# First row tiles by two PSUM tiles, early weights in four large pieces, and smaller moves in a fused attention and gated feed-forward kernel

## Chip, core, metric

One core of one Trainium2 chip. The metric is device time in microseconds (us) of one execution; every kernel was compared with the reference in each run and was correct. All executions used are with a granted TensorE clock of 0.998 to 1.0. PE is TensorE, DVE is VectorE, ACT is ScalarE and SP is SyncE; PSUM is where the kernel puts the results of its matmuls.

## The reference, cut to what matters

```python
xn = _layernorm(x)                      # x: 2048 x 640
s  = attention(xn @ wq, k, v) @ wo      # 32 heads of 192, last 512 keys
g  = silu((silu(xn @ w_gate) * (xn @ w_up)) @ w_down)     # F = 1536
return x + s * g
```

## The kernel before: the parts concerned

Rows are worked in 4 blocks of 4 tiles of 128. For block 0 the kernel normalizes each tile, transposes it by TensorE into PSUM, copies it to `xnT`, and starts the gate and up products (steps f = 0 to 2) tile by tile while weights still arrive. The rest of block 0 (f = 3 to 11) takes 512 columns at a time. Then come blocks 1 to 3, whose rows are transposed by DMA, and the 16 head pairs of the attention. A context is one head pair with one block of 512 rows; its matmuls are mostly row-tiled, that is, they come in pairs of 64 rows each.

```python
load_x(0)                  # in two halves, on SP's and ACT's queue
load_x(1, nc.scalar)
for cs in (slice(0, 1), slice(1, 3), slice(3, NC)):       # first quarter of w_gate, w_up
    if cs.stop == NC: load_x(2)
    for eng, w_sb, w in ((nc.sync, wg_sb, B_w_gate), (nc.scalar, wu_sb, B_w_up)): ...
load_x(3); load_gu(1)
for t in range(4, 8): load_x(t)
load_gu(2); load_gu(3); ...
# [cut]
def ready(t):
    ln_transpose(t)                                       # 5 chunks into one PSUM tile
    n = NC if t else 2
    nc.scalar.copy(xnT[:, 0:n, rows], tps[t][:, 0:n, :])
    if n < NC: nc.vector.tensor_copy(out=xnT[:, n:NC, rows], in_=tps[t][:, n:NC, :])
# [cut] in the loop over blocks b and steps f, for the next block's rows
if nx and 1 <= f < 5: ln_stats(4 * b + 3 + f) ...
if nx and 5 <= f < 9:
    ln_apply(4 * b + f - 1)
    ln_transpose_dma(4 * b + f - 1)
# [cut] attention: query projection of the next context; drop() does the last half
# of an output tile that was held back from the context before
for c in range(NC):
    if c == NC - 1 and between: between()
# [cut] division of a context: first query tile on DVE, second on ACT, if i < 2
```

The softmax here doesn't subtract the row's maximum and nothing guards it: scores larger than these inputs give would overflow.

Of the kernel before, what the change touches and what calls it, by code (L numbers as in the profile page):

```python
# [15 lines left out]
def kernel(  # L16
# [13 lines left out]
    nc = tc.nc  # L30
# [35 lines left out]
    wpool = ctx.enter_context(tc.tile_pool(name="att_w", bufs=2))  # L66
    kpool = ctx.enter_context(tc.tile_pool(name="att_k", bufs=1))
    qpool = ctx.enter_context(tc.tile_pool(name="att_q", bufs=2))
    psum = ctx.enter_context(tc.tile_pool(name="psum", bufs=2, space=bass.MemoryType.PSUM))

    def sc_tile():
        return psum.tile([P, 2, 512], f32, name="sc", tag="sc")

    def mm_tile():
        return psum.tile([P, 2, 512], f32, name="mm", tag="mm")


    ctx.enter_context(tc.manual_schedule())
# [86 lines left out]
    with ExitStack() as fctx:  # L165
# [13 lines left out]

        def load_x(t, eng=nc.sync):  # L180
            x_t[t] = lnx.tile([P, D], bf, name="x_t")
            if t == 0:
                for r, eng in ((lo, nc.sync), (hi, nc.scalar)):
                    eng.dma_start(out=x_t[t][r, :], in_=x2[t * P + r.start : t * P + r.stop, :])
            else:
                eng.dma_start(out=x_t[t][:], in_=x2[t * P : (t + 1) * P, :])

        def load_gu(q):
            cols = slice(q * FQ, (q + 1) * FQ)
# [4 lines left out]
                out=wu_sb[:, :, cols], in_=B_w_up[:, cols].rearrange("(c p) f -> p c f", p=P)  # L194
            )

        load_x(0)
        load_x(1, nc.scalar)
        for cs in (slice(0, 1), slice(1, 3), slice(3, NC)):
            if cs.stop == NC:  # L200
                load_x(2)
            for eng, w_sb, w in ((nc.sync, wg_sb, B_w_gate), (nc.scalar, wu_sb, B_w_up)):
                src = w[cs.start * P : cs.stop * P, 0:FQ].rearrange("(c p) f -> p c f", p=P)
                eng.dma_start(out=w_sb[:, cs, 0:FQ], in_=src)
        load_x(3)
        load_gu(1)
        for t in range(4, 8):
            load_x(t)
        load_gu(2)
        load_gu(3)  # L210
        nc.sync.dma_start(out=wd_sb[:], in_=B_w_down.rearrange("(f p) d -> p f d", p=P))


        nc.scalar.activation(act_t[:], one_t[:], ACT.Sqrt)
        warm = sc_tile()

        def keep_warm(n):
            for _ in range(n):
                nc.tensor.matmul(warm[:, 0, :], zero_t[:, 0:P], zero_t[:], start=True, stop=True)

        keep_warm(11)

        def ln_stats(t, between=None):
            b, ti = divmod(t, 4)
# [30 lines left out]
                    op0=ALU.subtract, op1=ALU.mult,  # L255
                )

        tps = {}

        def ln_transpose(t):  # L260
            xn = xns.pop(t)
            tps[t] = tp[:, t % 2, 0 : NC * P].rearrange("p (c k) -> p c k", c=NC)
            for c in range(NC):
                nc.tensor.transpose(tps[t][:, c, :], xn[:, c * P : (c + 1) * P], ident[:])

        def ln_transpose_dma(t):
            nc.sync.dma_start_transpose(
                out=xnT[:, 0:NC, t * P : (t + 1) * P], in_=xns.pop(t)[:]
            )
# [13 lines left out]
            nc.scalar.activation(sg[:], g, ACT.Silu)  # L283
            nc.vector.tensor_tensor(hTs[b][:, f, :], u, sg[:], ALU.mult)  # L284

        def ffn_hidden(b, f):
            gu = mm_tile() if (b, f) == (0, 3) else sc_tile()
            for s in range(2):
                hidden_mm(gu[:, s, :], s, f, slice(b * 512, (b + 1) * 512))
            hidden_gate(b, f, gu[:, 0, :], gu[:, 1, :])  # L290

        def ffn_down(b, u):
            ti, n = divmod(u, 2)
# [23 lines left out]
        hTs[0] = ffh.tile([P, NF, 512], bf, name="hT")  # L317


        first = {f: [sc[:, s, :] for s in range(2)] for f, sc in ((0, sc_tile()), (1, sc_tile()))}  # L320
        tp = psum.tile([P, 2, 1024], bf, name="tp", tag="mm")
        first[2] = [mm[:, s, :] for mm in (mm_tile(),) for s in range(2)]
        def ready(t):
            ln_transpose(t)
            rows = slice(t * P, (t + 1) * P)
            n = NC if t else 2
            nc.scalar.copy(xnT[:, 0:n, rows], tps[t][:, 0:n, :])
            if n < NC:
                nc.vector.tensor_copy(out=xnT[:, n:NC, rows], in_=tps[t][:, n:NC, :])

        ln_stats(0)
        ln_sqrt(0)
        ln_stats(1, lambda: ln_apply(0, (slice(0, 2 * P), slice(2 * P, D))))
        ready(0)
        ln_sqrt(1)
        keep_warm(3)
        banks = [(f, s) for f in range(3) for s in range(2)]
        for t in range(4):
            rows = slice(t * P, (t + 1) * P)

            order = [(*fs, [c]) for c in range(NC) for fs in banks]
            if t:
                order = [(*fs, range(NC)) for fs in banks]
            for k, (f, s, cs) in enumerate(order):
                if k == len(order) * 3 // 5 and t < 3:
                    if t == 1:
                        ln_stats(3, lambda: ln_apply(2))
                    else:
                        ln_apply(t + 1)
                    ready(t + 1)  # L350
                    if t == 0:
                        ln_stats(2)
                    if t < 2:
                        ln_sqrt(t + 2)
                    else:
                        nc.scalar.activation(act_t[:], one_t[:], ACT.Silu)
                hidden_mm(first[f][s][:, rows], s, f, rows, cs)
                if t == 3 and s == 1:
                    hidden_gate(0, f, *first[f])
        nc.gpsimd.memset(V_p[:, :, :, Dh : Dh + 2], 1.0)  # L360

        for b in range(NB):
            if b:
                hTs[b] = ffh.tile([P, NF, 512], bf, name="hT")
            nx = b + 1 < NB
            u = 0
            for f in range(NF):
                if nx and b and f == 0:
                    for t in range(4 * b + 4, 4 * b + 8):
                        load_x(t)  # L370
                if b or f >= 3:
                    ffn_hidden(b, f)
                if nx and 1 <= f < 5:
                    ln_stats(4 * b + 3 + f)
                    if f == 4:
                        ln_rstd(b + 1, 0, 4)
                if nx and 5 <= f < 9:
                    ln_apply(4 * b + f - 1)
                    ln_transpose_dma(4 * b + f - 1)

                if b >= 1 and f % 3:
                    ffn_down(b - 1, u)
                    u += 1
                if b == 2:
                    if f == 0:
                        load_k(0)
                    elif 2 <= f < 6:
                        transpose_k(0, f - 2)
                    elif f == 6:
                        load_wq(0)  # L390
                    elif 7 <= f < 10:
                        sum_k(0, f - 7)
                elif b == 3:
                    if f < 5:
                        centre_k(0, f)
                    elif f < 8:
                        (load_k, load_wq, load_wo)[f - 5]((1, 1, 0)[f - 5])
# [23 lines left out]
    def q_rows(i, j, between=None):  # L421
        pr, b = divmod(i, NB)
        if i not in qTs:
            qTs[i] = qpool.tile([P, 3, 512], bf, name="qT")
        q_ps = mm_tile()
        for c in range(NC):
            if c == NC - 1 and between:
                between()
            for h, r in enumerate((lo, hi)):
                nc.tensor.matmul(  # L430
                    q_ps[:, h, :], pairs[pr]["wq"][r, c, j * P : (j + 1) * P], xnT[r, c, b * 512 : (b + 1) * 512],
                    start=(c == 0), stop=(c == NC - 1),
                )
        with nc.allow_low_precision(reason="a sum of two, rounded once, like a copy out of PSUM"):
            nc.vector.reduce_sum(  # L435
                qTs[i][:, j, :], q_ps[:, :, :].rearrange("p h n -> p n h"), axis=AX.X
            )
# [13 lines left out]
    def pv(i, q2):  # L451
# [4 lines left out]
        def part(p):  # L456
            if p == 0:
                if q2 == 0:
                    Obs[i] = opool.tile([P, 4, 2, Dh], bf, name="O_b")
                    tag = "OT_l" if late(i) and pr < last else "OT_b"  # L460
                    OTs[i] = otpool.tile([P, 12, P], bf, name=tag, tag=tag, bufs=2 if tag == "OT_l" else 3)
                st["alone"] = i < 2 or (pr == last and 2 * b + q2 < 5)
                st["acc"] = sc_tile() if st["alone"] and q2 and b < 2 else mm_tile()
            acc = st["acc"]
            turn, h = divmod(p, 2)
            for kc in range(KC):
# [10 lines left out]
            if p == 1:  # L477
                turned(m, st)
            if p == 3:
                divide(i, q2, acc, st["alone"])  # L480

        return [lambda p=p: part(p) for p in range(4)]

    def divide(i, q2, acc, alone):
        pr, b = divmod(i, NB)
        O_b, OT_b = Obs[i], OTs[i]
        r = smpool.tile([P, 2, 2, 1], f32, name="r")
# [2 lines left out]
        for k in range(2):  # L490
            qt = 2 * q2 + k
            a_k = a_v[:, k, :, :]
            if k == 0 and alone:
                nc.vector.tensor_tensor(
                    O_b[:, qt, :, :], a_k[:, :, 0:Dh], r[:, k, :, :].to_broadcast([P, 2, Dh]),
                    ALU.mult,
                )
                continue
# [9 lines left out]
    def pv_full(i, q2):  # L508
# [4 lines left out]
            tag = "OT_l" if late(i) and pr < last else "OT_b"  # L513
            OTs[i] = otpool.tile([P, 12, P], bf, name=tag, tag=tag, bufs=2 if tag == "OT_l" else 3)
        O_b, OT_b = Obs[i], OTs[i]
        alone = i < 2 or (pr == last and 2 * b + q2 < 5)
        acc = sc_tile() if alone and b == 1 else mm_tile()
        for k in range(2):
            qt = 2 * q2 + k
            for h in range(2):  # L520
                for kc in range(KC):
# [2 lines left out]
                        Ps[i][kc][:, h, qt * P : (qt + 1) * P], V_p[:, kc, h, 0 : Dh + 1],  # L524
                        start=(kc == 0), stop=(kc == KC - 1),
                    )
        divide(i, q2, acc, alone)

    def load_xr(t):
        xrs[t] = finp.tile([P, D], bf, name="x_r", bufs=8)  # L530
# [243 lines left out]
```

## Time and profile before

| | before |
|---|---|
| median of 6 executions | 924.16 us (923.96 to 924.82) |
| the profiled one, its span | 924.28, 922.5 us |
| first matmul on real weights | 6.88 us |
| first 512-column matmul of block 0 | 15.69 us |
| PE busy from 203 to 915 us | 711.95 of 712.00 us |

A row of the order of time is start, duration (of a merged group: from its first start to its last end), engine, line, operation, tiles, count, and in brackets the idle time of the engine before it with what ended it. A row of the chain of waits is start, duration, and what the end of the program hung on just then. The records of matmuls overlap: 64-row ones of 512 columns are shown as 376 ns long, though pairs follow each other every 216 ns. Rows between those shown are left out of the fences.

### The profile page before, as it was taken

How to read it: one execution, taken by the hardware profiler on the slowest of the kernel's cores; microseconds unless marked ns; L12 is line 12 of the kernel's file. 1: busy time of each engine (PE TensorE's matmuls, PEld its weight loads, DVE VectorE, ACT ScalarE, POOL GpSimd, SP SyncE). 2: the span in 40 equal slices, each digit the busy share in tenths (PEclk: the TensorE clock that was granted, in tenths of full speed). 3: DMA queues.
4: the chain of work that ended last, by engine and by line, in shares of the span. 5: the costliest groups of instructions: out<-in, count | busy, mean ns of one | idle time of the engine just before them, and what ended most of it. 6: DMA issues, size and time to landing. Idle time of an engine off the chain costs nothing.

```text
span 922.5 us, 25778 instructions
## 1 busy us (share of the span) xinstructions
PE 915.9 (99%) x11085; PEld 624.4 (68%) x11101; DVE 575.7 (62%) x847; ACT 473.7 (51%) x847; POOL 101.6 (11%) x390
## 2 busy tenths in 40 slices
PE   9999999999999999999999999999999999999998
PEld 5455555575858586868686767676777777676666
DVE  6433331467676767676666667676767676767656
ACT  4222223556464656555556565655555555556561
POOL 0000000000000000000000000000000000002978
PEclk9999999999999999999999999999999999999999
DMA  9321510044544434444536262525271817163534
GB/s 293 78 53 35 114 35 1 1 74 93 88 78 83 83 79 88 72 93 65 102 57 109 55 112 53 113 45 121 41 125 36 131 37 123 32 124 92 120 71 141
DMA packets 243810, 77.18 MB, mean 84 GB/s; under 512 B 224624, under 2 KB 243696, under 8 KB 243696
## 3 DMA queue, kind: packets, MB, share of 16 engines
q1 hardware_dynamic: 242640, 74.73, 41.7%
q8 instruction: 87, 1.43, 0.7%
q10 hardware_dynamic: 1056, 0.80, 0.3%
q14 instruction: 27, 0.22, 0.1%
HBM read 39.45 MB, written 2.62 MB: 46 GB/s over the span
## 4 chain that ended last, share of the span: by engine, by line
PE 98%; DMA 1%; DVE 0%; ACTq 0%; issue 0%; POOLq 0%; POOL 0%; DVEq 0%
PE mm L430 22%; PE sc L567 19%; PE sc L444 18%; PE mm L470 16%; PE sc L276 11%; PE mm L298 6%; PE sc L539 3%; PE mm L522 2%; PE mm L539 1%; DMA wu_sb<-in_B_w_up_dram 1%; PE mm L276 0%; PE mm L311 0%; PE sc L470 0%; PE sc L522 0%; PE mm L444 0%
## 5 line engine op out<-in xcount | busy, mean ns | idle before, releaser
L448 ACT ACTIVATE p_t<-sc 128x1024 bf16<-128x1024 f32 x254 | 252.9, 1022 | 128.6 <-PE sc L444 128.6
L435 DVE TENSOR_REDUCE qT<-mm 128x512 bf16<-128x1024 f32 x189 | 231.0, 1223 | 92.5 <-PE mm L430 90.0
L500 ACT ACTIVATE O_b<-mm,r 128x192 bf16<-128x192 f32 x486 | 164.6, 421 | 183.4 <-issue 161.3
L430 PE MATMUL mm<-xnT,wq_p 64*128 64x512 bf16 x1890 | 240.1, 376 | 0.0
L592 DVE TENSOR_TENSOR sacc<-sacc,sc 128x640 f32<-128x640 f32 x200 | 164.3, 821 | 89.4 <-PE sc L567 89.4
L567 PE MATMUL sc<-wo_p,OT_b 64*128 64x320 bf16 x2592 | 217.2, 296 | 0.0
L444 PE MATMUL sc<-qT,khat 64*128 64x512 bf16 x1524 | 198.2, 376 | 0.1
L470 PE MATMUL mm<-V_p,p_t 64*128 64x193 bf16 x3520 | 186.3, 243 | 0.0
L470 PEld LDWEIGHTS <-p_t 64*128 64x128 bf16 x3584 | 162.6, 93 | 12.5 <-issue 0.4
L430 PEld LDWEIGHTS <-wq_p 64*128 64x128 bf16 x1890 | 105.2, 94 | 95.0 <-issue 0.5
L567 PEld LDWEIGHTS <-OT_b 64*128 64x128 bf16 x2592 | 140.1, 94 | 21.6
L444 PEld LDWEIGHTS <-khat 64*128 64x128 bf16 x1536 | 85.5, 94 | 79.4 <-issue 0.4
L555 POOL MEMSET turn_t<- 128x1 f32 x328 | 32.2, 98 | 696.4 <-PE mm L470 474.0
L284 DVE TENSOR_TENSOR hT<-sc,sg 128x512 bf16<-128x512 f32 x46 | 31.7, 690 | 85.2 <-ACT sg L283 85.1
L283 ACT ACTIVATE sg<-sc 128x512 bf16<-128x512 f32 x46 | 27.3, 596 | 72.4 <-PE sc L276 72.4
L276 PE MATMUL sc<-xnT,wu_sb 128*128 128x512 bf16 (+1 forms) x259 | 59.1, 355 | 0.3 <-DMA wu_sb<-in_B_w_up_dram 0.3
L276 PE MATMUL sc<-xnT,wg_sb 128*128 128x512 bf16 (+1 forms) x248 | 58.6, 354 | 0.6
L298 PE MATMUL mm<-wd_sb,hT 128*128 128x320 bf16 x384 | 56.6, 299 | 0.0
L489 DVE RECIPROCAL r<-mm 128x4 f32<-128x4 f32 x124 | 22.7, 183 | 47.4 <-PE mm L470 36.0
L298 PEld LDWEIGHTS <-hT 128*128 128x128 bf16 x384 | 37.5, 98 | 19.0
L276 PEld LDWEIGHTS <-wu_sb 128*128 128x128 bf16 x285 | 26.3, 98 | 27.2 <-DMA wu_sb<-in_B_w_up_dram 0.4
L276 PEld LDWEIGHTS <-wg_sb 128*128 128x128 bf16 x285 | 26.4, 98 | 23.2 <-DMA wg_sb<-in_B_w_gate_dram 0.2
(69 smaller groups left out, 373.8 us busy)
## 6 DMA issues: line engine op xcount, KB each, us to landing
wo_p<-in_A_wo_dram SPq DMA_DIRECT2D x16, 480.0 KB, 4.2
K_p<-in_A_k_cache_dram SPq DMA_DIRECT2D x32, 192.0 KB, 3.3
V_p<-in_A_v_cache_dram SPq DMA_DIRECT2D x32, 192.0 KB, 3.0
wq_p<-in_A_wq_dram SPq DMA_DIRECT2D x64, 80.0 KB, 3.1
wq_p<-in_A_wq_dram SPq DMA_DIRECT2D x16, 160.0 KB, 3.3
x_r<-in_A_x_dram SPq DMA_DIRECT2D x16, 160.0 KB, 4.1
x_t<-in_A_x_dram SPq DMA_DIRECT2D x14, 160.0 KB, 3.0
OT_b<-O_b SPq DMA_TRANSPOSE x124, 2.9
```

The costliest lines, as they stand in the source:

```text
L276: nc.tensor.matmul(out, w_sb[:, c, f * P : (f + 1) * P], xnT[:, c, qc], start=(c == 0), stop=(c == NC - 1),)
L298: nc.tensor.matmul(dn[:, 0:HD], hTs[b][:, f, ti * P : (ti + 1) * P], wd_sb[:, f, cols], start=(f == 0), stop=(f == NF - 1),)
L430: nc.tensor.matmul(q_ps[:, h, :], pairs[pr]["wq"][r, c, j * P : (j + 1) * P], xnT[r, c, b * 512 : (b + 1) * 512], start=(c == 0), stop=(c ...
L435: nc.vector.reduce_sum(qTs[i][:, j, :], q_ps[:, :, :].rearrange("p h n -> p n h"), axis=AX.X)
L444: nc.tensor.matmul(sc[:, h, :], khat[r, j, ks], qT[r, j, :], start=(j == 0), stop=(j == 2))
L448: nc.scalar.activation(p_t[:, :, :], sc[:, :, :], ACT.Exp, scale=scale)
L470: m = nc.tensor.matmul(acc[:, k, h * 256 : h * 256 + Dh + 1], Ps[i][kc][r, h, qt * P : (qt + 1) * P], V_p[r, kc, h, 0 : Dh + 1], start=(p ...
L500: nc.scalar.activation(O_b[:, qt, h, :], a_k[:, h, 0:Dh], ACT.Copy, scale=r[:, k, h, :])
L539: nc.tensor.matmul(ps, OTs[i][:, 3 * qt + j, :], pairs[i // NB]["wo"][:, j, cols], start=(first and j == 0), stop=(end and j == 2),)
L555: st["turn"] = nc.gpsimd.memset(turn_t[:], 0.0)
L567: m = nc.tensor.matmul(ps[:, n, 0:HD], OTs[i][r, 3 * qt + j, :], pairs[i // NB]["wo"][r, j, n * HD : (n + 1) * HD], start=(turn == 0 and j ...
L592: nc.vector.tensor_tensor(s_t, s_t, sc[:, :, 0:HD], ALU.add)
```

## The change

Its intent: let PE begin tile 0 after two of five transposes; fetch the early weights in fewer, larger transfers; put the weights of steps 6 to 8 ahead of rows not yet needed; and spare contexts 0 and 1 the hand-over from DVE to ACT within one division. With it come a new place for the transposes in a tile (four fifths), next block's layer norm one step later, and the held part one chunk earlier.

```diff
+        def load_first(cs):
+            for w_sb, w in ((wg_sb, B_w_gate), (wu_sb, B_w_up)):
+                nc.sync.dma_start(out=w_sb[:, cs, 0:FQ], in_=src)
-        load_x(0)
+        load_x(0, nc.scalar)
         load_x(1, nc.scalar)
-        for cs in (slice(0, 1), slice(1, 3), slice(3, NC)): ...
+        load_first(slice(0, 2))
+        load_first(slice(2, NC))
+        load_x(2)
         load_x(3)
         load_gu(1)
+        load_gu(2)
         for t in range(4, 8):
             load_x(t)
-        load_gu(2)
# [cut: pools; warming on zeros of 9 long and 6 short matmuls, none after the transposes]
+            for tp, cs in zip(tps, PARTS):        # chunks 0-1 and 2-4, a PSUM tile each
+                for k, c in enumerate(range(cs.start, cs.stop)):
+                    nc.tensor.transpose(tp[:, k, :], xn[:, c * P : (c + 1) * P], ident[:])
# [cut: copies by part on ACT; the last part of tile 3 on DVE]
-            if t:
+            if t == 3:
                 order = [(*fs, range(NC)) for fs in banks]
-                if k == len(order) * 3 // 5 and t < 3:
+                if k == len(order) * 4 // 5 and t < 3:
# [cut: step 3 ahead of the loop]
-                if nx and 1 <= f < 5:
-                    ln_stats(4 * b + 3 + f)
+                if nx and 2 <= f < 6:
+                    ln_stats(4 * b + 2 + f)
-                if nx and 5 <= f < 9:
+                if nx and 6 <= f < 10:
-            if c == NC - 1 and between:
+            if c == NC - 2 and between:
-                divide(i, q2, acc, st["alone"])
+                divide(i, q2, acc, (0, 1) if i < 2 and q2 == 0 else ())
```

More of the change, by code (lines that the diff above doesn't have):

```diff
@@ L68 @@
     qpool = ctx.enter_context(tc.tile_pool(name="att_q", bufs=2))
-    psum = ctx.enter_context(tc.tile_pool(name="psum", bufs=2, space=bass.MemoryType.PSUM))
+    sc_pool = ctx.enter_context(tc.tile_pool(name="psum_sc", bufs=2, space=bass.MemoryType.PSUM))
+    mm_pool = []
     def sc_tile():
-        return psum.tile([P, 2, 512], f32, name="sc", tag="sc")
+        return sc_pool.tile([P, 2, 512], f32, name="sc")
     def mm_tile():
-        return psum.tile([P, 2, 512], f32, name="mm", tag="mm")
+        return mm_pool[0].tile([P, 2, 512], f32, name="mm")
     ctx.enter_context(tc.manual_schedule())
@@ L181, in load_x @@
             x_t[t] = lnx.tile([P, D], bf, name="x_t")
-            if t == 0:
-                for r, eng in ((lo, nc.sync), (hi, nc.scalar)):
-                    eng.dma_start(out=x_t[t][r, :], in_=x2[t * P + r.start : t * P + r.stop, :])
-            else:
-                eng.dma_start(out=x_t[t][:], in_=x2[t * P : (t + 1) * P, :])
+            eng.dma_start(out=x_t[t][:], in_=x2[t * P : (t + 1) * P, :])
+        def load_first(cs):
+            for w_sb, w in ((wg_sb, B_w_gate), (wu_sb, B_w_up)):
+                src = w[cs.start * P : cs.stop * P, 0:FQ].rearrange("(c p) f -> p c f", p=P)
+                nc.sync.dma_start(out=w_sb[:, cs, 0:FQ], in_=src)
         def load_gu(q):
@@ L195, in load_gu, with keep_warm @@
             )
-        load_x(0)
+        load_x(0, nc.scalar)
         load_x(1, nc.scalar)
-        for cs in (slice(0, 1), slice(1, 3), slice(3, NC)):
-            if cs.stop == NC:
-                load_x(2)
-            for eng, w_sb, w in ((nc.sync, wg_sb, B_w_gate), (nc.scalar, wu_sb, B_w_up)):
-                src = w[cs.start * P : cs.stop * P, 0:FQ].rearrange("(c p) f -> p c f", p=P)
-                eng.dma_start(out=w_sb[:, cs, 0:FQ], in_=src)
+        load_first(slice(0, 2))
+        load_first(slice(2, NC))
+        nc.scalar.activation(act_t[:], one_t[:], ACT.Sqrt)
+        load_x(2)
         load_x(3)
         load_gu(1)
+        load_gu(2)
         for t in range(4, 8):
             load_x(t)
-        load_gu(2)
         load_gu(3)
         nc.sync.dma_start(out=wd_sb[:], in_=B_w_down.rearrange("(f p) d -> p f d", p=P))
-        nc.scalar.activation(act_t[:], one_t[:], ACT.Sqrt)
-        warm = sc_tile()
-        def keep_warm(n):
-            for _ in range(n):
-                nc.tensor.matmul(warm[:, 0, :], zero_t[:, 0:P], zero_t[:], start=True, stop=True)
-        keep_warm(11)
+        early = ExitStack()
+        psum1 = early.enter_context(tc.tile_pool(name="psum1", bufs=1, space=bass.MemoryType.PSUM))
+        PARTS = (slice(0, 2), slice(2, NC))
+        tps = [psum1.tile([P, 8, P], bf, name="tp", tag="tp%d" % n) for n in range(2)]
+        first = [
+            [gu[:, s, :] for s in range(2)]
+            for gu in (sc_tile(), sc_tile(), psum1.tile([P, 2, 512], f32, name="gu"))
+        ]
+        def keep_warm(n, cols=512):
+            for _ in range(n):
+                nc.tensor.matmul(
+                    first[2][1][:, 0:cols], zero_t[:, 0:P], zero_t[:, 0:cols], start=True, stop=True
+                )
+        keep_warm(9)
+        keep_warm(6, P)
         def ln_stats(t, between=None):
@@ L256, in ln_apply @@
                 )
-        tps = {}
-        def ln_transpose(t):
-            xn = xns.pop(t)
-            tps[t] = tp[:, t % 2, 0 : NC * P].rearrange("p (c k) -> p c k", c=NC)
-            for c in range(NC):
-                nc.tensor.transpose(tps[t][:, c, :], xn[:, c * P : (c + 1) * P], ident[:])
         def ln_transpose_dma(t):
@@ L284, in hidden_gate, with ffn_hidden @@
             nc.vector.tensor_tensor(hTs[b][:, f, :], u, sg[:], ALU.mult)
-        def ffn_hidden(b, f):
-            gu = mm_tile() if (b, f) == (0, 3) else sc_tile()
+        def ffn_hidden(b, f, gu=None):
+            gu = gu or [sc[:, s, :] for sc in (sc_tile(),) for s in range(2)]
             for s in range(2):
-                hidden_mm(gu[:, s, :], s, f, slice(b * 512, (b + 1) * 512))
-            hidden_gate(b, f, gu[:, 0, :], gu[:, 1, :])
+                hidden_mm(gu[s], s, f, slice(b * 512, (b + 1) * 512))
+            hidden_gate(b, f, *gu)
         def ffn_down(b, u):
@@ L317 @@
         hTs[0] = ffh.tile([P, NF, 512], bf, name="hT")
-        first = {f: [sc[:, s, :] for s in range(2)] for f, sc in ((0, sc_tile()), (1, sc_tile()))}
-        tp = psum.tile([P, 2, 1024], bf, name="tp", tag="mm")
-        first[2] = [mm[:, s, :] for mm in (mm_tile(),) for s in range(2)]
         def ready(t):
-            ln_transpose(t)
-            rows = slice(t * P, (t + 1) * P)
-            n = NC if t else 2
-            nc.scalar.copy(xnT[:, 0:n, rows], tps[t][:, 0:n, :])
-            if n < NC:
-                nc.vector.tensor_copy(out=xnT[:, n:NC, rows], in_=tps[t][:, n:NC, :])
+            xn, rows = xns.pop(t), slice(t * P, (t + 1) * P)
+            for tp, cs in zip(tps, PARTS):
+                for k, c in enumerate(range(cs.start, cs.stop)):
+                    nc.tensor.transpose(tp[:, k, :], xn[:, c * P : (c + 1) * P], ident[:])
+            for tp, cs in zip(tps, PARTS):
+                part = tp[:, 0 : cs.stop - cs.start, :]
+                if t == 3 and cs.stop == NC:
+                    nc.vector.tensor_copy(out=xnT[:, cs, rows], in_=part)
+                else:
+                    nc.scalar.copy(xnT[:, cs, rows], part)
         ln_stats(0)
@@ L335 @@
         ln_sqrt(1)
-        keep_warm(3)
         banks = [(f, s) for f in range(3) for s in range(2)]
@@ L359 @@
                     hidden_gate(0, f, *first[f])
+        ffn_hidden(0, 3, [psum1.tile([P, 512], f32, name="gu3", tag="tp%d" % n)[:, :] for n in range(2)])
+        early.close()
+        mm_pool.append(ctx.enter_context(tc.tile_pool(name="psum_mm", bufs=2, space=bass.MemoryType.PSUM)))
         nc.gpsimd.memset(V_p[:, :, :, Dh : Dh + 2], 1.0)
@@ L370 @@
                         load_x(t)
-                if b or f >= 3:
+                if b or f >= 4:
                     ffn_hidden(b, f)
-                if nx and 1 <= f < 5:
-                    ln_stats(4 * b + 3 + f)
-                    if f == 4:
+                if nx and 2 <= f < 6:
+                    ln_stats(4 * b + 2 + f)
+                    if f == 5:
                         ln_rstd(b + 1, 0, 4)
-                if nx and 5 <= f < 9:
-                    ln_apply(4 * b + f - 1)
-                    ln_transpose_dma(4 * b + f - 1)
+                if nx and 6 <= f < 10:
+                    ln_apply(4 * b + f - 2)
+                    ln_transpose_dma(4 * b + f - 2)
                 if b >= 1 and f % 3:
@@ L461, in part @@
                     OTs[i] = otpool.tile([P, 12, P], bf, name=tag, tag=tag, bufs=2 if tag == "OT_l" else 3)
-                st["alone"] = i < 2 or (pr == last and 2 * b + q2 < 5)
-                st["acc"] = sc_tile() if st["alone"] and q2 and b < 2 else mm_tile()
+                st["acc"] = sc_tile() if i < 2 and q2 else mm_tile()
             acc = st["acc"]
@@ L479, in part, with divide @@
             if p == 3:
-                divide(i, q2, acc, st["alone"])
+                divide(i, q2, acc, (0, 1) if i < 2 and q2 == 0 else ())
         return [lambda p=p: part(p) for p in range(4)]
-    def divide(i, q2, acc, alone):
+    def divide(i, q2, acc, by_dve):
         pr, b = divmod(i, NB)
@@ L492, in divide @@
             a_k = a_v[:, k, :, :]
-            if k == 0 and alone:
+            if by_dve and k in by_dve:
                 nc.vector.tensor_tensor(
@@ L515, in pv_full @@
         O_b, OT_b = Obs[i], OTs[i]
-        alone = i < 2 or (pr == last and 2 * b + q2 < 5)
+        alone = pr == last and 2 * b + q2 < 5
         acc = sc_tile() if alone and b == 1 else mm_tile()
@@ L526, in pv_full @@
                     )
-        divide(i, q2, acc, alone)
+        divide(i, q2, acc, alone and (0,))
     def load_xr(t):
```

## The prediction

> **What bounds the kernel now.** I read the page's shares first, then busy time by stretch, then the chain of waits, then the order of time of the first 36 us and of the stretch round 195 us. A stretch's columns are length, then busy us (instructions) of PE, PEld, DVE, ACT, POOL, then the granted clock, DMA share and GB/s.
>
> ```profile
> PE 915.9 (99%) x11085; PEld 624.4 (68%) x11101; DVE 575.7 (62%) x847; ACT 473.7 (51%) x847; POOL 101.6 (11%) x390
> ...
> 0.00:6.88 6.88, 5.41 (x19) 2.04 (x20) 3.27 (x13) 2.12 (x5) 0.79 (x8) 1.00 0.60 176
> 6.88:15.69 8.81, 8.51 (x137) 7.75 (x136) 4.25 (x13) 4.28 (x9) 0.00 (x0) 1.00 1.08 342
> ...
> 203.00:915.00 712.00, 711.95 (x9630) 508.74 (x9626) 488.40 (x677) 402.22 (x724) 92.22 (x363) 1.00 0.46 86
> ```
>
> PE's 99% alone would prove little, but from 203 to 915 us it is busy 711.95 of 712.00 us at full clock. The change removes no matmul of that stretch, so what is to be had lies in the head of the program: 6.88 us before the first real matmul (what PE does there is warming on zeros and five transposes), and 8.81 us in which the first four row tiles are worked. After that a gain is kept only if PE meets no new wait.
>
> In the first row tile the order of time shows the path:
>
> ```profile
> 5.36 0.64 DVE L253 TENSOR_SCALAR xn<-x_t,mv,rstd 128x256 bf16<-128x256 bf16 x2
> 5.76 0.63 PE L264 MATMUL tp<-ident,xn 128*128 128x128 bf16 x5 [0.24 <-DVE xn L253]
> 6.43 0.37 ACT L327 COPY xnT<-tp 128x256 bf16<-128x256 bf16 x1 [1.30 <-PE tp L264]
> 6.88 0.22 PE L276 MATMUL sc<-xnT,wg_sb 128*128 128x128 bf16 x1
> 7.95 0.23 PE L276 MATMUL sc<-xnT,wu_sb 128*128 128x128 bf16 x1 [0.30 <-DMA wu_sb<-in_B_w_up_dram]
> 9.05 0.69 ACT L327 COPY xnT<-tp 128x640 bf16<-128x640 bf16 x1 [2.05 <-PE tp L264]
> 9.79 0.44 PE L276 MATMUL sc<-xnT,wg_sb 128*128 128x128 bf16 x5
> ```
>
> The copy of two chunks starts only when all five transposes of the one PSUM tile are done (6.39), though its two were done near 6.05. Then PE stops at 7.42 for a weight piece until 7.95, and near 9.0 for another. The tiles after the first begin at 9.79, 11.91 and 14.02: 2.11 us each. The chain of waits names the same transfer, issued at 2.43 and landed 5.47 us later:
>
> ```profile
> 2.43 5.47 DMA wu_sb<-in_B_w_up_dram
> ...
> 195.54 0.79 PE mm L470 x16
> 196.33 0.67 PE sc L470 x16
> ...
> 199.41 0.79 PE mm L470 x16
> ```
>
> Its later lines show the only two visible losses of pair 0: two runs of 16 matmuls take 0.79 us where the others take 0.67, so 0.12 us each.
>
> **What the Trainium skill says.** "TensorE: Matmul & The Clock Gate", section "Wait — 56ns, not 53.3ns?", gives 55.6 and 215.7 ns from start to start for warm matmuls of 128 and 512 columns. The trace agrees (starts at 9.41, 9.47, 9.52; five 512-column ones from 17.85 to 18.93), so I count 0.056 and 0.216 us. "DMA: Bandwidth & Descriptors", section "Issuing engines are not separate DMA queues", says transfers of both issuing engines share the same 16 DMA engines, so moving the weights to one queue buys no bandwidth. The stretch agrees: 342 GB/s from 6.88 to 15.69 us with both queues and later with SP's alone. "Perfetto Trace Analysis", section "DMA Optimizations", says both that larger transfers fill the bandwidth better and that splitting lets some begin sooner: the choice here, for this trace to settle.
>
> **The change, part by part.**
>
> *Head of tile 0.* Two PSUM tiles let the first copy follow the second transpose: 6.05 + 0.04 = 6.09, plus 0.37 and 0.08 to the matmul (6.80 to 6.88 before), gives 6.54: 0.34 us earlier. This keeps x's landing and so 5.76 as they are, though x now comes in one piece on one queue. The three warming matmuls go as well, but those ended before the copy mattered. The second copy (384 columns on ACT, 0.48 us between 0.37 and 0.69) ends near 6.95, before the 12 matmuls on two chunks are through (6.54 + 12 x 0.056 = 7.21).
>
> *Weights.* All four pieces and x 0 and 1 are 960 + 320 = 1280 KB. Transfers begin near 2.0 us, and some 505 KB are through by 4.0. At 340 KB per us the rest would be through at 6.3; but in the trace landings trail: nothing lands between 4.62 and 7.38, and the piece at a like place in the order (third of w_up, 192 KB) lands at 8.41. So the last piece lands between 6.7 and 8.5, and I take 7.5. It is needed at 7.21 plus 0.06: 0.25 us of waiting instead of the 0.47 + 0.16 before.
>
> *Tiles 0 to 3.* Transposes come at four fifths of a tile. Tile 0: 30 x 0.056 + 5 x 0.056 = 1.96 us, so without a weight wait it ends at 8.50. Copy of tile 1's first two chunks: transposes start at 7.88, two of them with latency 0.28, then 0.04, 0.37 and 0.05: 8.62, a wait of 0.12, much like today's. The period stays 2.1 us for tiles 1 and 2 (xn of tile 2 is ready near 9.95, when PE reaches it at 9.96). Tile 3 starts near 12.9 and, with its second copy on DVE, runs 1.73 us: end near 14.63 against 15.69, a gain of 1.06. Less 0.25 for the weights: about 0.8 us.
>
> *Second quarter before x 4 to 7, and layer norm of the next block one step later.* The weights of steps 3 to 11 brought no wait before, so their move gains nothing. But each of steps 3 to 11 takes 2.16 us, and the last normalization of block 1's rows is moved from behind the gate of step 8 to that of step 9:
>
> ```profile
> 29.47 0.69 DVE L284 TENSOR_TENSOR hT<-sc,sg 128x512 bf16<-128x512 f32 x1 [1.11 <-ACT sg L283]
> 30.08 0.44 DVE L253 TENSOR_SCALAR xn<-x_t,mv,rstd 128x640 bf16<-128x640 bf16 x1
> 31.63 0.69 DVE L284 TENSOR_TENSOR hT<-sc,sg 128x512 bf16<-128x512 f32 x1 [1.11 <-ACT sg L283]
> ...
> 35.11 1.24 PE L276 MATMUL sc<-xnT,wg_sb 128*128 128x512 bf16 x5
> ```
>
> On before's clock it would run from 32.24 to 32.68; the transposing DMA is issued 0.02 later and lands 2.58 us after (the median of its kind), at 35.28, when PE wants it at 35.11. With 0.05 to wake PE that is a NEW WAIT of some 0.2 us at block 1. Both sides move with the head's gain, so the gain does not cure it. One of the four such DMAs here took 3.77 us; if the last did, the wait would be 1.4 us. I count 0.25. Blocks 2 and 3 have the down projection between steps and slack of us.
>
> *First contexts divided by one engine each.* In context 0 and 1 today ACT starts its half only after DVE's (194.05 + 0.56, ACT at 194.71), ends at 195.44, and PE's next use of that PSUM buffer starts at 195.49: 0.11 late; again 0.13 at 199.36. With both DVE divisions for the first half the buffer is free near 195.09 and 198.84: both waits go, 0.24 us. But the second half now takes four ACT divisions (1.35 us, as at 207.92) after a reciprocal that DVE reaches later: 198.94 to 200.40. The second output tile of context 2 takes that PSUM buffer, wanted at 200.43 - 0.24 = 200.19: a wait of about 0.25 us. Net nothing.
>
> *The held part one chunk earlier in the query projection.* It changes the order of matmuls in a stretch with no idle PE: nothing.
>
> Sum: -0.8 + 0.25 + 0 = about -0.6 us, so 924.18 - 0.6 = 923.6.
>
> **Rivals.** (1) *All of it shows*: the pieces land before 7.2, no wait at block 1, pair 0 gives 0.24: -1.3, so 922.9. For it speaks that a single queue runs at 350 GB/s after 8 us; against it, the landings that trail and the 2.58 us of the transposing DMA. (2) *The weights wait as long as before*: larger pieces finish later, the last at 8.5, PE stands for 1.2 us in tile 0; then the head gains 0.1, block 1 loses 0.25: 924.3. For it speaks the hole between 4.62 and 7.38, whose cause the trace does not give: DMA share was only 0.6 to 0.8 there, so something other than bandwidth held them, and fewer pieces may cure it. (3) *The slow transposing DMA falls on the last*: 1.2 us more, 924.8; a chance of perhaps one in ten. (4) *PE cools down*: the gap between warming and transposes grows from 0.24 to about 0.5 us; in before no idle of this size changed the pace of matmuls, so I give this little.
>
> **Range and chances.** The whole that can move is below 1.5 us of 924, 0.2%; 2% would be 18 us. The three times of before spread over 0.4 us. From rivals 1 and 2 with that spread: 922.7 to 924.4 should hold it 8 times in 10. Within 2% is all but certain: faster 0.005, same 0.99, slower 0.005.
>
> **What would show it.** Right: first matmul on real weights near 6.5 us; one wait for a weight transfer below 0.5 us in tile 0; block 0's first 512-column matmul near 14.8 instead of 15.69; a PE idle of 0.2 us on a transposing DMA near 34.3; no 0.79 at pair 0's second context, but a wait near 200 for ACT's division. Wrong: x 0 landing much after 3.6 us (all of the head shifts), the last weight piece after 8.2, no wait at block 1, or a change of PE's busy share between 203 and 915 us, which I hold fixed.

## The result, and the profile after

The changed kernel takes 923.10 us in the median of 6 (922.87 to 923.70) against 924.16 of 6 for before. The ratio is 0.9988, 95% interval 0.9976 to 1.0001; at a threshold of 2% that is "same". Ratios here are the mean time of one kernel's runs over that of the other's of the same rounds, so not quite the ratio of the medians. The profiled execution took 923.55, 0.73 under the profiled one of before.

The stretches of the changed kernel, with the columns of the prediction:

```profile
6.88:15.69 8.81, 8.34 (x134) 7.62 (x133) 4.66 (x14) 4.90 (x14) 0.00 (x0) 1.00 1.09 337
15.69:35.11 19.42, 19.24 (x89) 8.61 (x89) 12.46 (x27) 5.78 (x11) 1.27 (x2) 1.00 0.69 180
...
203.00:915.00 712.00, 712.00 (x9627) 510.34 (x9624) 488.87 (x677) 401.95 (x722) 92.89 (x364) 1.00 0.46 86
```

These say little: PE is as busy as before, and the middle one is less busy. The head in order of time says more:

```profile
5.75 0.63 PE L326 MATMUL tp<-ident,xn 128*128 128x128 bf16 x5 [0.72 <-DVE xn L262]
6.07 0.82 ACT L332 COPY xnT<-tp 128x256 bf16<-128x256 bf16 x2 [0.96 <-PE tp L326]
6.49 0.22 PE L277 MATMUL sc<-xnT,wg_sb 128*128 128x128 bf16 x1
7.16 0.22 PE L277 MATMUL sc<-xnT,wg_sb 128*128 128x128 bf16 x1
7.79 0.23 PE L277 MATMUL sc<-xnT,wu_sb 128*128 128x128 bf16 x1 [0.41 <-DMA wu_sb<-in_B_w_up_dram]
...
15.01 1.24 PE L277 MATMUL gu<-xnT,wg_sb 128*128 128x512 bf16 x4
```

ACT now starts its first copy at 6.07, not 6.43, and the first real matmul comes at 6.49, not 6.88. From 7.16 to 7.79 PE does nothing new: it waits for the last weight piece (0.63 less the 0.056 that one matmul takes: 0.58). The 512-column matmuls begin 0.68 us earlier. The start of block 1, same view:

```profile
31.56 0.44 DVE L262 TENSOR_SCALAR xn<-x_t,mv,rstd 128x640 bf16<-128x640 bf16 x1
33.36 1.24 PE L277 MATMUL sc<-xnT,wu_sb 128*128 128x512 bf16 x5
34.73 1.24 PE L277 MATMUL sc<-xnT,wg_sb 128*128 128x512 bf16 x5
```

Five matmuls of 0.216 us from 33.36 end their turn at 34.44, but the next starts at 34.73: 0.29 us lost, after the transposing DMA that was issued at 32.02 and landed at 34.59. The view prints no wait, since the records of the matmuls before run on until 34.60.

The rest of the balance is in the chain of waits. First the changed kernel round pair 0, then before and changed at the start of pair 1:

```profile
195.15 0.67 PE mm L474 x16
...
198.89 0.67 PE mm L474 x16
199.56 0.99 PE sc L571 x12
```

```profile
210.78 0.42 PE sc L567 x6
211.20 0.02 issue
211.22 0.84 DVE sacc L590
212.06 0.04 issue
212.10 0.82 PE sc L444 x6
```

```profile
210.09 0.41 PE sc L571 x6
210.50 0.43 PE mm L435 x4
210.93 1.31 PE sc L449 x12
```

Both runs of 0.79 have become 0.67, and one run of 12 output matmuls takes 0.99 where others take 0.81. In before, the chain at 211.22 goes through DVE: the held output tile leaves PSUM late, and the second score tile of pair 1 waits for its buffer. I hadn't looked at that row. In the changed kernel it is gone.

The same by stretches, each from the starts of three matmuls that both programs have (the differences are worked out from the traces):

| | before | changed | difference |
|---|---|---|---|
| first 512-column matmul of block 0 | 15.69 | 15.01 | -0.68 |
| from there to the first row-tiled query projection | 152.62 | 152.91 | +0.29 |
| from there to the last pair's first value product | 675.80 | 675.50 | -0.30 |

Sum -0.69, which is the difference of the spans (922.49 and 921.77 us) but for 0.03.

### The profile page after: what moved, and what is told of

Read it like the earlier page. It is cut to its first block, busy times and chain, and to the rows that moved or that the text cites. A ratio compares the mean times of both kernels' runs of the same rounds, so it can differ in the third digit from the quotient of the medians.

```text
span 921.8 us, 25768 instructions
## 1 busy us (share of the span) xinstructions
PE 914.4 (99%) x11086; PEld 625.7 (68%) x11102; DVE 576.0 (62%) x847; ACT 474.0 (51%) x850; POOL 101.5 (11%) x390
## 4 chain that ended last, share of the span: by engine, by line
PE 98%; DMA 1%; POOL 0%; DVE 0%; issue 0%; SPq 0%; POOLq 0%; DVEq 0%
PE mm L435 22%; PE sc L571 19%; PE sc L449 18%; PE mm L474 16%; PE sc L277 11%; PE mm L299 6%; PE sc L543 2%; PE mm L526 2%; DMA wu_sb<-in_B_w_up_dram 1%; PE gu L277 0%; DMA out_dram<-ob 0%; PE mm L543 0%; PE mm L312 0%; PE sc L474 0%; PE sc L526 0%; POOL ob L631 0%
```

## Experiments

All twelve ran beside the kernel before. E below is the start of the first 512-column matmul of block 0, R that of the first real matmul.

**1. The changed kernel again.** No edit.

> The changed kernel unchanged, as the yardstick for the other runs on this chip. Its six times so far spread over 0.83 us (922.87 to 923.70), those of before over 0.86, and the profiled one (923.55) is 0.73 us under the profiled one of before. Theory: the difference is a sum of fixed terms (head -0.68, block 1 +0.29, pair 0 -0.08, held part -0.23 = -0.70) and what varies beyond that is when the fourth weight piece lands (7.75 us in the profiled run). Then this profile again has the first real matmul at 6.49 and block 1's wait of 0.29 to within 0.05, and only the weight wait differs from 0.58. Rival: the landing is fixed too and the spread is noise elsewhere: weight wait 0.58 again, within 0.05.

Measured 923.04 us (922.89 to 923.43, 5 executions); before 924.17. R 6.55, weight wait 0.61, E 15.10, block 1's wait 0.28, pair 0's 0.15: these waits are fixed to 0.03; R came 0.06 later, with x 0. So the rival (the landing is fixed too) held here, within 0.05: the landing repeated (7.83), and this run alone could not say what the spread is. The runs below that keep these transfers could: in five of them the last piece landed at 7.11 to 7.56.

**2. Next block's layer norm one step earlier, as before.**

```diff
-  if nx and 2 <= f < 6: ln_stats(4 * b + 2 + f)      +  if nx and 1 <= f < 5: ln_stats(4 * b + 3 + f)
-  if nx and 6 <= f < 10: ... (4 * b + f - 2)         +  if nx and 5 <= f < 9: ... (4 * b + f - 1)
```

> The changed kernel with the layer norm of the next block put back one step earlier, everything else as changed. Theory: the last transposing DMA of block 1's rows is what PE waits for at 34.73 us (0.29 us); one step of 2.16 us earlier it lands near 32.5 and the wait is gone, with nothing else moved: 0.29 us faster than the changed kernel. Rival: x 4 to 7 now land later (15.1 to 16.7 us), so statistics one step earlier push DVE's gates and PE waits for a PSUM buffer near step 6 instead: gain below 0.1 us, and a new idle of PE between 19 and 24 us.

Measured 923.25 us (922.91 to 924.72). Block 1's wait is gone, and the rival's idle came, 0.28 us at step 6, so that the second stretch of the table takes 152.90 as in the changed kernel (the last row is of a view that ends at 22.0):

```profile
18.87 0.21 DVE L241 BATCH_NORM_AGGREGATE mv<-stats 128x2 f32<-128x12 f32 x1
19.87 0.21 DVE L241 BATCH_NORM_AGGREGATE mv<-stats 128x2 f32<-128x12 f32 x1
20.32 1.24 PE L277 MATMUL sc<-xnT,wu_sb 128*128 128x512 bf16 x5
20.86 0.21 DVE L241 BATCH_NORM_AGGREGATE mv<-stats 128x2 f32<-128x12 f32 x1
20.99 0.64 DVE L285 TENSOR_TENSOR hT<-sc,sg 128x512 bf16<-128x512 f32 x1
21.68 0.59 PE L277 MATMUL sc<-xnT,wg_sb 128*128 128x512 bf16 x2
```

DVE does three tiles' statistics in a row before the gate of step 4 (20.99 to 21.63), which frees the PSUM buffer that step 6 wants at 21.40. The rival had the place right and the reason wrong: DVE waits for no x here, so the late landing is not the cause. It is the order of DVE's work, because step 3's gate now stands ahead of those statistics. The later layer norm of the change thus isn't careless: it avoids one wait of 0.28 and pays another of 0.29.

**3. Tile 0's transposes in one PSUM tile, tiles 1 to 3 as changed.**

```diff
+  places = [(tps[0], cs.start) for cs in PARTS] if t == 0 else [(tp, 0) for tp in tps]
```

> The changed kernel with the transposes of row tile 0 in one PSUM tile again; tiles 1 to 3 keep two. The first copy should wait for all five transposes, and the first real matmul go from 6.49 to about 6.85. Theory A: in this program the weight piece that lands at 7.75 sets the end of tile 0, so the earlier start is swallowed by that wait: wait 0.2 instead of 0.58, the first 512-column matmul again at 15.01, no change of the time (within 0.05 in the trace). Rival B, the working of my prediction: the 0.34 us of the earlier start carries through to the end: 0.34 us slower. Rival C: the copy does not wait for the other transposes at all, and nothing moves.

Measured 923.26 us (923.17 to 924.06). R 6.90, as expected, but E 14.83, earlier than the changed kernel's profile:

```profile
5.68 0.75 PE L327 MATMUL tp<-ident,xn 128*128 128x128 bf16 x5
6.90 0.22 PE L277 MATMUL sc<-xnT,wg_sb 128*128 128x128 bf16 x1 [0.46 <-ACT xnT L333]
```

The last piece landed at 7.26 in this run and PE waited for no weights. So the copy does wait for all five transposes (rival C falls), but the run doesn't decide between A and B: the landing moved by 0.5 us, more than the term in dispute. Run 11 settles it.

**4. Before, with only the held part one chunk earlier.**

```diff
-            if c == NC - 1 and between:
+            if c == NC - 2 and between:
```

> The kernel before with one line changed: the held last half of an output tile one chunk earlier in the query projection. My prediction gave it nothing. Theory now: before loses 0.23 us at 212.10 us, where the second score tile of pair 1 waits for DVE to move the held tile out of PSUM; with the half 0.216 us earlier the wait all but goes: 0.2 us faster than before, all of it between 211 and 212.2 us, nothing elsewhere. Rival: a matmul record was merely missing there, and nothing changes (under 0.03 us in the trace).

Measured 923.76 us (923.66 to 924.49), before 924.17; ratio 0.9997 (0.9984 to 1.0011), which decides nothing. The chain does:

```profile
195.16 0.79 PE mm L470 x16
...
210.18 0.41 PE sc L567 x6
210.59 0.43 PE mm L430 x4
211.02 1.31 PE sc L444 x12
```

DVE has left the chain at 211 us, the rest (the 0.79) is as before, and the last stretch of the table takes 675.58 instead of 675.80: 0.22 us won by this line alone.

**5. The changed kernel with the early transfers of before.** x 0 in halves, pieces of 1, 2 and 2 chunks on two queues, as in the code above.

> The changed kernel with the early transfers of before: x 0 in halves on two queues, weights of the first quarter in three pieces of 1, 2 and 2 chunks on two queues; two PSUM tiles and the new order stay. In four profiles of the changed head the first 512-column matmul of block 0 stood at 14.83 to 15.10 us, in two of the head of before at 15.31 and 15.69. Theory: the head's gain comes from the pieces, as what PE waits for in tile 0 is the last one's landing (7.26 to 7.83 us in four pieces, 8.69 to 8.97 in six). Then here the last piece lands at 8.6 to 9.0 and that matmul stands at 15.3 to 16.0. Rival: the two PSUM tiles and the interleaved order carry the gain: 15.1 or earlier. Either way block 1's wait stays near 0.29.

Measured 924.72 us (923.67 to 926.89, 4 executions), before 924.20. R 6.53, E 16.46:

```profile
6.53 0.22 PE L282 MATMUL sc<-xnT,wg_sb 128*128 128x128 bf16 x1
7.85 0.23 PE L282 MATMUL sc<-xnT,wg_sb 128*128 128x128 bf16 x1 [0.83 <-DMA wg_sb<-in_B_w_gate_dram]
9.52 0.23 PE L282 MATMUL sc<-xnT,wg_sb 128*128 128x128 bf16 x1 [0.69 <-DMA wg_sb<-in_B_w_gate_dram]
```

The early start is worth nothing here: PE stands 0.99 and 0.85 us for weights, the last piece landing at 9.48. It was later than I had expected (8.6 to 9.0), and E later than the range. The theory stands and the rival falls: in this run, without the new transfers, the PSUM tiles and the new order gain nothing. Block 1's wait is 0.23. The times spread over 3.2 us, the widest here, and only the profiled execution's landings are known.

**6. Pieces of 2, 2 and 1 chunks on the one queue.**

```diff
-        load_first(slice(2, NC))
+        load_first(slice(2, NC - 1))
+        load_first(slice(NC - 1, NC))
```

> The changed kernel with the weights of the first quarter in pieces of 2, 2 and 1 chunks instead of 2 and 3. PE can then work chunks 2 and 3 while the last is under way. Theory A: the wait for the last piece (0.58 and 0.61 us in two profiles) is pure loss, so all of it is won: wait in tile 0 below 0.1, first 512-column matmul near 14.5. Theory B: behind the weights the rows of tile 2 land (8.2 us) and need 2.2 us of statistics, root and normalization (8.23 to 10.37), which PE reaches at 10.49 now; so the wait goes from tile 0 but comes back before the transposes of tile 2: the matmul stands at 14.8 to 15.0, no more than 0.15 us won. If smaller pieces land later as a whole, it is later than 15.1.

Measured 922.88 us (922.87 to 923.17, 4 executions), before 924.20. E 14.44, no wait for weights:

```profile
6.51 0.22 PE L278 MATMUL sc<-xnT,wg_sb 128*128 128x128 bf16 x1
7.17 0.22 PE L278 MATMUL sc<-xnT,wg_sb 128*128 128x128 bf16 x1
7.23 0.22 PE L278 MATMUL sc<-xnT,wu_sb 128*128 128x128 bf16 x1
```

Where the changed kernel stops after 7.16, the stream runs on. Theory B fell for a reason I hadn't counted on: the pieces themselves landed earlier, the last at 6.93, and tile 2's rows at 7.36 instead of 8.20, with the same bytes ahead of them. One profile can't tell this from a lucky landing: with four pieces too the last one landed as early as 7.11 (run 12). Over all profiles, PE stood over 0.3 us for the last piece in three of the seven with four pieces (changed, runs 1 and 7) and in none of the four with 2, 2 and 1.

**7. Second halves of contexts 0 and 1 shared by DVE and ACT.**

```diff
-  divide(i, q2, acc, (0, 1) if i < 2 and q2 == 0 else ())
+  divide(i, q2, acc, ((0, 1), (0,))[q2] if i < 2 else ())
```

> The changed kernel, but in the second halves of contexts 0 and 1 DVE divides the first of two query tiles and ACT the other, as before; the first halves stay DVE's alone. Theory: PE's new wait of 0.155 us at 199.96 is for the PSUM buffer that ACT's four divisions hold until 200.4 on the clock of before; with DVE (0.56) then ACT (two, 0.73) it is free some 0.15 earlier and the wait is below 0.05: 0.12 us faster from 190 to 203 us, and the wait of before at the first half stays away. Rival: DVE's division delays its reciprocals, and PE waits elsewhere as long.

Measured 923.30 us (923.05 to 924.09, 4 executions), before 924.20. The wait is 0.18 instead of 0.155; the theory is refuted:

```profile
198.38 0.56 DVE L498 TENSOR_TENSOR O_b<-sc,r 128x384 bf16<-128x384 f32 x1
199.03 0.73 ACT L504 ACTIVATE O_b<-sc,r 128x192 bf16<-128x192 f32 x2 [3.01 <-DVE O_b L498]
```

ACT starts only after DVE is done, so 0.65 and 0.73 stand one after the other: 1.38 us, against 1.35 for ACT alone in the changed kernel (198.56 to 199.91, PE starting again at 199.96). Sharing one tile between two engines gave no overlap at all, which is what the change had set out to avoid.

**8. Statistics as changed, two of four normalizations at step 6.**

```diff
-  if nx and 6 <= f < 10:  (one tile: 4 * b + f - 2)
+  if nx and 6 <= f < 9:
+      for t in ((4, 5), (6,), (7,))[f - 6]:
```

> The changed kernel with the statistics of the next block where the change put them (steps 2 to 5), but two of the four normalizations at step 6, so that the last comes at step 8 as before. Putting everything one step earlier removed block 1's wait and brought one of 0.28 us at step 6 (21.68 us), as DVE had three statistics between the gates of steps 3 and 4. Theory: that wait was DVE's order, so here neither comes: the last transposing DMA lands near 32.5 us, PE wants it at 34.44, first matmul of block 1 without wait, 0.29 us less from 15.0 us to block 1. Rival: the extra normalization at step 6 delays gate 7 and a wait of 0.1 to 0.3 us appears between 26 and 30 us.

Measured 922.62 us (922.53 to 922.80, 4 executions), before 924.20; ratio 0.9982 (0.9967 to 0.9997). Neither wait came:

```profile
32.84 1.24 PE L277 MATMUL sc<-xnT,wu_sb 128*128 128x512 bf16 x5
33.91 1.24 PE L277 MATMUL sc<-xnT,wg_sb 128*128 128x512 bf16 x5
```

33.91 is 32.84 plus 5 x 0.216, and the second stretch of the table is 152.62 again, 0.29 less than changed. The head is that of the changed kernel, yet E is 14.49: the last piece landed at 7.14 and no weight was waited for.

**9. Runs 6 and 8 together.**

> The changed kernel with both gains together: weights of the first quarter in pieces of 2, 2 and 1 chunks, and the next block's normalizations ending one step earlier. Theory: they are independent and land on different waits, so the trace has no weight wait in tile 0 (first 512-column matmul near 14.45) and none at block 1; only pair 0's wait of 0.15 stays. The end is 0.29 under that of the 2-2-1 run's trace (921.03): span near 920.7, and its times bunch closer than those of the changed kernel, which spread with the landing of the last piece: near 922.5, a spread below 0.4. Rival: the head's 14.44 was a lucky landing (the run with only the normalization moved had 14.49 with the old pieces), and this run's matmul stands anywhere between 14.4 and 15.1.

Measured 922.89 us (922.80 to 923.27, 5 executions), before 924.28. Neither wait is there (152.62), and the span is 921.02. E is 14.64, not 14.45: x 0 landed at 3.84 and R is 6.70. My expected spread of 0.4 was also missed (0.47). The two gains hold side by side in the trace, but by the times this version is no better than run 8.

**10. As 9, with ACT on the first half of context 1 and DVE on the second.**

```diff
-  (0, 1) if i < 2 and q2 == 0 else ()
+  (0, 1) if i < 2 and q2 == i else ()
```

> As the run with both gains, and in context 1 the engines changed over: ACT divides the first half alone, DVE the second. Theory: the wait at the second output tile of context 2 (0.15 us) is for the second half's buffer alone; with DVE it is free 0.5 earlier and the wait goes; ACT's first half then ends about 0.1 after PE wants that buffer, so 0.10 at the start of the second value product instead: 0.05 us faster from 190 to 203 us, not to be seen in the times. Rival: the waits add up, 0.15 stays and 0.1 comes.

Measured 922.84 us (922.65 to 923.12), before 924.28.

```profile
198.08 0.77 PE mm L476 x16
198.85 0.81 PE sc L573 x12
```

The 0.99 is 0.81 again, and the 0.10 came where it was expected. The last stretch takes 675.43 against 675.50: 0.07 won, invisible in the times.

**11. As 9, with tile 0 in one PSUM tile.** The edit of run 3.

> As the run with both gains, with the transposes of row tile 0 in one PSUM tile. In the changed kernel this cost nothing to be seen, as PE would have waited for weights anyway (first real matmul 6.90 instead of 6.49 to 6.55, yet the 512-column matmul at 14.83). Theory: where the weights no longer bind, the first copy does: 0.34 us slower, first 512-column matmul near 14.8 against 14.45. Rival: something else in the head binds (statistics of tile 2), and it is again within 0.1.

Measured 923.03 us (922.92 to 923.19), before 924.28. R 6.90, E 14.83, against 6.70 and 14.64 of run 9, 6.56 and 14.49 of run 10:

```profile
6.90 0.22 PE L278 MATMUL sc<-xnT,wg_sb 128*128 128x128 bf16 x1 [0.46 <-ACT xnT L334]
```

E less R is 7.93 or 7.94 in all these, in runs 3, 8 and 12 too: without a weight wait, E follows R one to one. Against runs 9 and 10 the difference is 0.19 and 0.34, as run 9 had x late and run 10 had not. From the first transpose to R it is 1.22 us here and 0.74 in both of them; of this excess 0.12 is PE's slow pace, since these transposes still ran at 0.107 us (run 7, as slow, has 0.86 with two tiles). So the split is worth 0.36 us where weights are there in time.

**12. Rows 4 to 7 ahead of the weights of steps 6 to 8, as before.** (The texts call these weights, `load_gu(2)`, the second quarter; they are the third.)

```diff
         load_gu(1)
-        load_gu(2)
         for t in range(4, 8):
             load_x(t)
+        load_gu(2)
```

> The changed kernel with rows 4 to 7 of x loaded ahead of the second weight quarter, as before. Theory: neither is waited for (in the changed profile they land at 15.1 to 16.7 and 13.2 to 14.7 us and are first used near 18.1 and 21.5), so the order gives nothing: no wait of PE between 15 and 34 us, block 1's wait 0.29 as ever, and the head anywhere in its spread of 14.5 to 15.1. Rival: the quarter then lands after PE wants it, and PE waits near 21.5 us.

Measured 923.25 us (922.84 to 924.14, 4 executions), before 924.28. No wait between 15 and 34 us, block 1's at 0.285, second stretch 152.90 as changed: this part of the change gives nothing.

## Why the prediction was right, and where not

*The head, -0.8 predicted, -0.68 in the profile.* The mechanism is the one given. R was to be 6.54 and is 6.49. The term mis-sized is the weights: I took a landing at 7.5 and a wait of 0.25; it was 7.75 and 0.58. The tiles' working erred the other way and hid half of that: from R to E without a weight wait it has 8.09 us (14.63 less 6.54), and 7.93 was measured. Two relations fit all profiles with the changed order but run 5's to 0.05: E = landing + 7.27 where the last piece lands more than 12 matmuls (0.67 us) after R (changed, runs 1 and 7), else E = R + 7.93. With this head six profiles gave E from 14.49 to 15.10, mean 14.83 (changed, runs 1, 2, 7, 8, 12); the head of before gave 15.69 and 15.31 in two. So the profile of the result was one of the later ones, and the mean gain is 0.67 with two samples on one side. What of it is the transfers' and what the split's depends on the landing of the run: by the first relation the split only lengthened a wait in the changed profile, in run 11 it was worth 0.36.

Three readings of the prediction for the head were wrong. The last of the three warming matmuls did not end before the copy mattered: it kept PE from 6.67 to 6.88, when the first real one came, which cost some 0.02 us (from the copy's end to R it is 0.08 in the two profiles with that warming, 0.05 in the other twelve). The DMA share of the hole between 4.62 and 7.38 was low only at its start: 0.57 to 0.84 from 4.5 to 6.0, but 0.90 to 1.03 from 6.0 to 7.5. And "moving the weights to one queue buys no bandwidth" was taken from a stretch after 6.88; before that, the new transfers brought much more. From 4 to 5 us, before moved 159 GB/s and the changed kernel 346.

*Block 1, +0.25 predicted, +0.29.* As worked out: last normalization to 32.00, DMA issued at 32.02, landed 2.57 later. Runs 2 and 8 show that the step is the cause, run 8 that it was not needed. Both sides did move with the head.

*Pair 0, 0 predicted, -0.08.* Both old waits went (-0.24, of which I read 0.12 each from the chain), and the new one for ACT's four divisions came at the place named, 0.155 instead of 0.25. From context 1's first division to the end of ACT's four I had 2.48 us (197.92 to 200.40), and 2.50 was measured (197.41 to 199.91). The error is in what else moves: I took both old waits off PE's time, but left these divisions on the clock of before, though the first wait's going (0.12) moves them too. Run 10 shows that it is this buffer.

*The held part, 0 predicted, -0.22.* This step was wrong. It rested on "a stretch with no idle PE", and the share of 711.95 in 712.00 was read as proof. But a matmul record runs on past the start of the next, so a wait of 0.23 us leaves 0.05 of idle, all of the 0.05 in that window. The chain of waits had a row for DVE there in the profile of before; run 4 shows that the one line removes it.

*Weights of steps 6 to 8 ahead of x ("second quarter"), 0 predicted.* Right by run 12.

*The sum.* -0.6 predicted, -0.69 in the profiles, -1.06 between the medians. The 0.13 too much for the head and the 0.22 missed at pair 1 nearly cancelled, so the total was nearer than its parts. Of the rivals, the second's delay of the weights came in part; the third (a slow last transposing DMA) showed in none of the runs, though the second or third of the four took 3.6 to 4.4 us; the fourth did not happen: the pace stayed full once reached. The remaining 0.4 between profiles and medians isn't shown to have a cause; the interval of the ratio (-2.2 to +0.1 us) covers it, and landings that differ by 0.7 us from run to run are a likely part of it.

*Open.* Why 1440 KB (x 0 to 2 and the first quarter) are complete at 8.7 to 9.5 us with x in halves and pieces of 1, 2, 2 on two queues, at 7.56 to 8.28 in four pieces on one, and at 7.2 to 7.6 in six pieces of 2, 2, 1 on one. The rate shows where it goes: from 4 to 5 us the three profiles with the transfers of before (before, runs 4 and 5) moved 143 to 174 GB/s, the eleven others 331 to 370, with four pieces or with six. So the sizes are not what makes this hole. Whether it is the halves of x, the two queues, the order, or ACT's table load, which falls into the same us in those three, is not known, as run 5 undid all of them together. No run undid the shorter warming, the four fifths or the order by chunks in tiles 1 and 2 alone.

## What to carry to other kernels

Judge a saturated TensorE by start-to-start times and the chain of waits, not by its busy share: overlapping records hide waits of two tenths of a us. When a chain is shortened or work is moved, ask at once which transfer, normalization or buffer was only just in time: here the earlier start met the last weight piece (0.58 us), the moved normalizations made block 1 wait (0.29), and the divisions moved to ACT held a PSUM buffer (0.155). Look at the rate of the first transfers too, not only at that of the stretch in which they are waited for. Two engines that share one output tile may run one after the other; before splitting work between them, look whether the second really starts early.

## What the Trainium skill lacked or had wrong

- "Perfetto Trace Analysis", section "Identifying the Most-Contended Engine", warns that TensorE's busy share misleads because pipelined instructions look smaller in the trace. In these views, where the ends of matmuls are modelled, they look larger: 376 ns for matmuls whose pairs start every 216, so a wait of 0.23 us showed 0.05 of idle.
- "TensorE: Matmul & The Clock Gate", section "What you observe", puts the change of pace around 4 us into activity, within 0.5 us. The spread here is wider. The first matmul is at 1.23 us in all profiles; the pace was full by 4.1 us in the changed kernel (2.9 after it) and by 4.8 in before (3.6), but in run 3, with no pause of PE until 5.9, two transposes were still 0.106 us apart at 6.02 (4.8 after it).
- "DMA: Bandwidth & Descriptors", section "Rules for kernel authors", advises larger transfers and says that more queues gain nothing. No page gives a loss at a program's start such as this: with x 0 in halves and the weights on two queues the core moved 143 to 174 GB/s from 4 to 5 us, with all weights on one queue 331 to 370, and the same 1440 KB took until 9.48 us in run 5 and 7.36 in run 6, whose pieces are smaller than those of the changed kernel (8.20).
- "ScalarE: Activation LUTs", section "What ACT_TABLE_LOAD costs", gives about 1.28 us for the load and 1.38 more for a drain. The load agrees (1.28 us), but no drain is seen on either side of it: in before it starts at 13.98, 0.02 us after the copy ahead of it has ended, and the next activation follows 0.02 us after its end, at 15.28.
